# Attention scores as four 64x64 quarters without one block, and v's transfer issued first in its slot

## The chip, the cores and the metric

The kernel runs on one core of a Trainium2 chip. The metric is the device time of one execution in microseconds (us), taken as the median of several runs.

## The reference, cut to what matters

A linear attention with a decay per channel (4 batches, 8 heads, 768 steps, head size 48) feeds a soft mixture of experts (8 experts with 4 slots each, hidden size 1024). Everything is 32-bit floating point.

```python
for t in range(S):                                   # S = 768
    cur = einsum('bhd,bhe->bhde', u * kt, vt)
    y[:, :, t] = einsum('bhd,bhde->bhe', rt, state + cur)
    state = wt[..., None] * state + einsum('bhd,bhe->bhde', kt, vt)
x = y.transpose(0, 2, 1, 3).reshape(B * S, H * D)    # 3072 x 384
logits = x @ phi                                     # 3072 x 32
d = softmax(logits, axis=0); c = softmax(logits, axis=1)
h = relu((d.T @ x)[e] @ w1[e]); slot_out[e] = h @ w2[e]
out = c @ slot_out
```

Step t reads the state of the steps before it, and its own key and value with the factor u. In chunks of 128 steps, the part inside a chunk is a product of scores: a key takes part for a query only if it is earlier than the query. So a 128 x 128 block of scores (keys down, queries across) is used above the diagonal alone, and of its four 64 x 64 quarters the one of late keys and early queries is not used at all.

## The kernel before

The work goes through 16 slots, n = 0 to 15, and a last one that only finishes (n = 16). A slot is one pair of heads of one batch: batch b = n // 4, pair j = n % 4. On the partitions, the two heads of a pair lie at rows 0 to 47 and 64 to 111. The kernel's order on each engine is the order in which the program writes it; no scheduler moves anything.

For each slot TensorE does, in this order: transposes of k (`b_kn`, L558); the output of the slot before, from the states (`c_inter`, L625) and from the scores and v (`c_av`, L634); the bonus with u (`b_bonus`, L583, not in slots with j = 3); the sums of k and v per chunk (`b_u`, L591, which reads the slot's v); and the scores in two halves of three chunks (`b_scores`, L569). Between the halves stand pieces of the experts' routing (L73, L77, L109 to L120). In slot 0 the first half of the scores stands ahead of the transposes, and where j is 2 the sums stand behind the first half.

A half of the scores is six matmuls: for each of three chunks and each of two heads, 48 rows, 128 keys as weights and 128 queries as moving columns. The heads use different row halves of the array and different banks of `ap`. The trace records each 32-bit matmul as two weight loads and two matmuls. Behind each half ScalarE copies `ap` (`b_at`, L574), GpSimd sets all but the part above the diagonal to zero (L576), and `c_av` of the next slot reads the result, in quarters of 64 weight columns.

VectorE makes the decayed keys and queries by scans (L526 to L544) for one unit of heads after another, ahead of their use. SyncE issues all DMAs, in program order; an issue that has to wait holds back those behind it. At a slot's head it issues, where the slot has them: the gather of the fourth pair's rows (`a_gather`, L511), which waits for VectorE; w of a later unit (`a_load_w`, L499), and its k and r (`a_load_kr`, L503); v of the next slot (`v_load`, L506), into one of three buffers; and pieces of the experts' weights (`weight_piece`, L670). At the kernel's start VectorE clears some tiles (L701 to L706) before its first scan.

After slot 16 come the last softmax, both expert layers and the mixing (L895 onward); a second program behind a test (`recompute`) is not entered.

Of the kernel before, what the change touches and what calls it, by code (L numbers as in the profile page):

```python
# [17 lines left out]
P = 128  # L18
# [3 lines left out]
B, H, S, D = 4, 8, 768, 48  # L22
# [3 lines left out]
NIT = B * NG  # L26
# [7 lines left out]
PIT = P + 1  # L34
# [15 lines left out]
def rwkv_soft_moe(ctx: ExitStack, tc: tile.TileContext, wc, krc, vc, cst, w1, w2, out):  # L50
    nc = tc.nc
# [397 lines left out]
    ap = [app[:, n] for n in range(2)]  # L449
# [38 lines left out]
    def Kt(n):  # L488
        b, g = divmod(n, NG)
        t = kr4[(NU * b + g) % 4] if g < NU else kr3  # L490
        return t[:, 0:RO]

    def Rt(n):
        b, g = divmod(n, NG)
        t = kr4[(NU * b + g) % 4] if g < NU else kr3
        return t[:, RO:KRW]

    def a_load_w(u):
        nc.sync.dma_start(out=ws[u % 2], in_=wc[u])  # L499

    def a_load_kr(u):
        for lo, hi in ((0, RO), (RO, KRW)):
            nc.sync.dma_start(out=kr4[u % 4][:, lo:hi], in_=krc[u][:, lo:hi])  # L503

    def v_load(n):
        nc.sync.dma_start(out=vts[n % 3].rearrange("p c h d -> p (c h d)"), in_=vc[n])  # L506

    def a_gather(u):
        s = u % NU
        for h in range(2):  # L510
            nc.sync.dma_start(out=kr3[64 * h + 16 * s:64 * h + 16 * s + 16, :],  # L511
                              in_=kr4[u % 4][64 * h + D:64 * h + 64, :])
# [10 lines left out]
    def a_back(u, lo=0, hi=ROW):  # L523
        w = ws[u % 2]
        n = (hi - lo) // PIT
        nc.vector.tensor_tensor_scan(out=G[:, lo:hi][:, ::-1], data0=w[:, lo:hi][:, ::-1],  # L526
                                     data1=g_one.broadcast_to([P, hi - lo]),
                                     initial=1.0, op0=ALU.mult, op1=ALU.min)
        nc.vector.reciprocal(out=holes(w, lo, n), in_=holes(Gp, lo + 1, n))
        if hi == ROW:  # L530
            later.append(lambda: nc.gpsimd.tensor_copy(out=chk[:, u, 0, :], in_=holes(w, 0)))
# [5 lines left out]
    def a_fwd(u, lo=0, hi=ROW):  # L537
        nc.vector.tensor_tensor_scan(out=G[:, lo:hi], data0=ws[u % 2][:, lo:hi],  # L538
                                     data1=g_zero.broadcast_to([P, hi - lo]),
                                     initial=1.0, op0=ALU.mult, op1=ALU.add)  # L540

    def a_r(u, lo=0, hi=ROW):
        r = kr4[u % 4][:, RO + lo:RO + hi]
        nc.vector.tensor_tensor(out=r, in0=r, in1=G[:, lo:hi], op=ALU.mult)  # L544
# [4 lines left out]
    def b_pat(n):  # L549
        src = holes(Kt(n), PIT, C - 1)  # L550
        nc.scalar.copy(out=pats[n % 2][:, :, 1:C],
                       in_=src.rearrange("p (o c) -> p o c", o=1).broadcast_to([P, D, C - 1]))
# [11 lines left out]
    def b_scores(n, hf):  # L564
        kt, rt = Kt(n), Rt(n)
        for cc in range(3):
            c = 3 * hf + cc
            for h in range(2):
                nc.tensor.matmul(  # L569
                    out=ap[h][:, cc * P:(cc + 1) * P], lhsT=kt[64 * h:64 * h + D, c * PIT + 1:c * PIT + PIT],  # L570
                    rhs=rt[64 * h:64 * h + D, c * PIT:c * PIT + P], start=True, stop=True)

    def b_at(n, hf):
        nc.scalar.copy(out=ats[n % 2][hf].rearrange("p h c t -> p h (c t)"), in_=app[:, :, 0:384])  # L574
# [20 lines left out]
    def b_a(n):  # L595
        if n % NG < NU:
            nc.scalar.copy(out=asb[n % 2], in_=aP)
# [76 lines left out]
    def weight_piece():  # L674
        for n, a in [next(pieces, (None, None))]:
            if n is None:
                return
            if n < E:
                in_halves(wa[n], w1[n], a * F, (a + 1) * F)
            else:  # L680
                in_halves(wa[n], w2[n - E], FT * COLS[a][0], FT * COLS[a][1])
# [22 lines left out]
    nc.vector.memset(g_zero, 0.0)  # L704
    nc.vector.memset(siT[:, 0:8], 0.0)
    nc.vector.memset(tp[0], 0.0)  # L706
    nc.gpsimd.memset(ones, 1.0)
    for n in range(2):
        nc.gpsimd.memset(pats[n], 0.0)
# [14 lines left out]
    for n in range(NIT + 1):  # L724
        b, j = divmod(n, NG)
        live = n < NIT
        m, l = n - 1, n - 2
        lb, lj = divmod(l, NG)
        sb_ = b - 1
        soft = live and 0 <= sb_ < B - 1  # L730

        u_next = NU * (b + 1) + j - 1
        if n == 0:
            a_load_w(2)
            a_load_kr(2)
        if j == 1 and live:
            a_gather(NU * b)
        if j in (1, 2) and live:
            a_gather(NU * b + j)
        if j >= 1 and u_next < B * NU and live:  # L740
            a_load_w(u_next)
            a_load_kr(u_next)
        if n + 1 < NIT:
            v_load(n + 1)
        if live:
            for _ in range(PIECES[n]):
                weight_piece()

        u0 = NU * b
        nxt = b + 1 < B  # L750
        if live:
            b_pat(n)
            if n == 0:
                a_back(1)
            elif j == 0:
                a_fwd(u0 + 1)
                a_r(u0 + 1)
                a_chk(u0 + 1)
            elif j == 1 and b:
                a_k(u0 + 2)  # L760
                a_fwd(u0 + 2)
            elif j == 2 and nxt:
                a_back(u0 + 3)
            elif j == 3 and nxt:
                a_r(u0 + 3)
                a_chk(u0 + 3)
        if n == NIT:
            q = qs[b - 2]
            sp0 = tp[0][0:TG, 0:DM]
            s_mm(xb[b % 2], q, sp0)  # L770
            l_turn(l, app)
            l_mm(0, xTs[0], lpv, True, False)
            s_acc(b - 2, q, sp0)
            s_sum(b - 2, q)
            s_rows_exp(q)
            s_norm(b - 2, q)

        if n == 0:
            b_scores(n, 0)
            b_at(n, 0)  # L780
        if live:
            b_kn(n)
        if m >= 0:
            c_inter(m)
            c_av(m)
            c_evac(m, n == NIT)
        if live:
            b_bonus(n)
        if n == 0:
            a_rk(1)  # L790
        elif live and j != 1 and (j == 0 or nxt):
            a_rk(u0 + (2 if j == 0 else j + 1))
        if live:
            if n == 1:
                keep_warm(2, tp[1])
            if j != 2:
                b_u(n)
            if n:
                b_scores(n, 0)
                b_at(n, 0)  # L800
            if j == 2:
                b_u(n)
            b_state(n)
            b_a(n)
        if j == 0 and b > 1 and live:
            q = qs[b - 2]
            s_mm(xb[b % 2], q, spv)
            s_acc(b - 2, q, spv)
            s_sum(b - 2, q)
        if soft and j == 1:  # L810
            l_mm(0, xTs[0], lpv, True, False)
            l_mm(1, xTs[1], lpv, False, True)
            nc.scalar.copy(out=lt_t, in_=lpv)
        if soft and j == 2:
            l_mm(2, xTs[0], lpv, True, True)
            nc.vector.tensor_tensor(out=lt_t, in0=lt_t, in1=lpv, op=ALU.add)
            qs[sb_] = q = s_max(sb_, lt_t)
        if soft and j == 3:
            s_turns(qs[sb_], dpv, lnv)

        if live:
            if n == 0:
                a_k(1)
                a_fwd(1)
                a_r(1)
                a_chk(1)
            if j == 0:
                a_back(u0 + 2)
            elif j == 1:
                if b == 0:  # L830
                    a_k(u0 + 2)
                    a_fwd(u0 + 2)
                a_r(u0 + 2)
                a_chk(u0 + 2)
            elif j == 2 and nxt:
                a_k(u0 + 3)
                a_fwd(u0 + 3)
            elif j == 3 and nxt:
                a_back(u0 + 4)
                a_k(u0 + 4)  # L840
        if live:
            b_tc(n)
        if l >= 0 and lj >= 1 and live:
            l_turn(l, ypp)
        if n == 1:
            keep_warm(4, tp[1])
        if live:
            b_scores(n, 1)
            if n == 1:
                keep_warm(2, tp[1])  # L850
            b_at(n, 1)
            b_av(n)
            while later:
                later.pop(0)()
            if n == 0:
                a_rk(2)
                keep_warm(9, yb[0])
        if soft and j == 2:
            s_exp(sb_, q)
        if j == 0 and 1 < b and live:  # L860
            s_rows_exp(qs[b - 2], nc.gpsimd)
        if j == 1 and 1 < b:
            ce = qs[b - 2]["ce"]
            nc.scalar.activation(out=ce, in_=ce, func=AF.Exp)
            s_norm(b - 2, qs[b - 2], nc.gpsimd)
# [205 lines left out]
```

## Time and profile before

| what | value |
|---|---|
| runs | 202.03 us median of 3 (192.95 to 204.23) |
| profiled execution | 194.6 us, its span 192.7 us |
| granted TensorE clock over the span | 0.955 |
| DMA | 52.12 MB, 270 GB/s over the span |
| slots 0 to 2 | to about 34 us |
| slots 3 to 15 | about 34 to 134 us |
| the last slot, experts and mixing | 134 to 192.7 us |

The profile is of one execution. Its span is from the first to the last instruction; the execution's time has 1.9 us more around it. PE is TensorE's matmuls and PEld its weight loads, which overlap them. In the chain of waits each row is a start, a length and what ended last there. "issue" is time in which an engine stood without waiting for anything that the profile shows. SPq is SyncE's queue of DMA issues. The queue q8 of the DMA table carries instructions, not data.

### The profile page before, as it was taken

The numbers are of one execution on the slowest core, as the hardware profiler recorded it, in microseconds if no ns is written. First come the engines' busy times: TensorE is split into PE (matmuls) and PEld (weight loads), VectorE is DVE, ScalarE is ACT, GpSimd is POOL, SyncE is SP. The second block draws the span as 40 slices with busy tenths as digits, with TensorE's granted clock in tenths as the row PEclk, the third lists the DMA queues.
The fourth block names the chain that finished last, engine by engine and source line by source line (L and its number), as shares of the span: only waits on it lengthen the run. The fifth ranks groups of instructions, "written<-read, shape, count | busy, mean of one in ns | idle before, by whom it ended". The sixth has DMA issues, their size and how long they took to land.

```text
span 192.7 us, 7876 instructions
## 1 busy us (share of the span) xinstructions
PE 169.2 (88%) x3393; PEld 126.5 (66%) x3397; DVE 110.1 (57%) x181; ACT 83.5 (43%) x187; POOL 87.5 (45%) x129
## 2 busy tenths in 40 slices
PE   6969999798899997999789999999979898998650
PEld 2464878787878984878679688896433225787450
DVE  4889497889564994947977691425431400124520
ACT  4233165375394672665546648674030201022420
POOL 5354667966639876539486576567000000000000
PEclk9975999999999999999999999999999999999955
DMA  5996748999999899999969998999995593008672
GB/s 135 340 323 177 200 154 221 379 385 376 246 373 310 305 316 376 255 383 275 340 197 336 354 266 228 315 379 377 363 360 173 209 264 121 0 3 359 260 284 99
DMA packets 23849, 52.12 MB, mean 270 GB/s; under 512 B 2944, under 2 KB 6784, under 8 KB 23808
## 3 DMA queue, kind: packets, MB, share of 16 engines
q1 hardware_dynamic: 23808, 51.55, 80.3%
q8 instruction: 28, 0.46, 1.1%
q14 instruction: 13, 0.11, 0.2%
HBM read 44.44 MB, written 4.72 MB: 255 GB/s over the span
## 4 chain that ended last, share of the span: by engine, by line
PE 74%; DMA 11%; DVE 4%; issue 3%; ACT 3%; POOL 0%; SPq 0%; DVEq 0%; ACTq 0%; POOLq 0%
PE ap L569 13%; PE y L634 10%; DMA v<-in_vc_dram 9%; PE G L197 6%; PE y L230 5%; PE y L625 5%; PE tp L591 5%; PE tp L558 4%; PE tp L583 4%; PE tp L77 3%; PE y L73 3%; PE ap L253 2%; PE tp L120 2%; DMA krb<-in_krc_dram 2%; PE y L687 2%
## 5 line engine op out<-in xcount | busy, mean ns | idle before, releaser
L576 POOL TENSOR_SCALAR_AFFINE_SELECT blkat<-blkat 128x768 f32<-128x768 f32 x32 | 27.7, 866 | 37.6 <-ACT blkat L574 28.4
L574 ACT COPY blkat<-ap 128x768 f32<-128x768 f32 x32 | 25.7, 802 | 29.0 <-PE ap L569 27.4
L634 PE MATMUL y<-v,blkat 128*64 128x48 f32 x768 | 26.1, 224 | 0.0
L569 PE MATMUL ap<-krb 48*128 48x128 f32 x288 | 23.7, 295 | 1.9 <-issue 1.4
L634 PEld LDWEIGHTS y<-v,blkat 128*64 128x64 f32 x768 | 23.8, 138 | 1.1
L569 PEld LDWEIGHTS ap<-krb 48*128 48x128 f32 x288 | 18.9, 192 | 5.9 <-ACT blkat L574 2.6
L526 DVE TENSOR_TENSOR_SCAN G<-blkw,G 128x774 f32<-128x774 f32 (+1 forms) x13 | 21.3, 1637 | 1.5 <-DMA blkw<-in_wc_dram 1.3
L538 DVE TENSOR_TENSOR_SCAN G<-blkw,G 128x774 f32<-128x774 f32 (+1 forms) x13 | 21.5, 1651 | 0.5
L519 POOL TENSOR_TENSOR blka<-krb 128x768 f32<-128x768 f32 x11 | 17.1, 1554 | 1.2 <-DMA krb<-in_krc_dram 1.2
L600 DVE TENSOR_TENSOR_SCAN Traw<-tp,blkm 112x288 f32<-112x288 f32 x16 | 12.1, 754 | 9.0 <-PE tp L591 9.0
L647 DVE TENSOR_TENSOR x<-y,av 128x288 f32<-128x288 f32 x17 | 7.6, 452 | 12.7 <-ACT x L644 11.5
L616 POOL TENSOR_TENSOR av<-v,asb 128x576 f32<-128x576 f32 x12 | 14.1, 1178 | 0.0
L591 PE MATMUL tp<-v,blkm 128*48 128x48 f32 x320 | 11.2, 215 | 3.1 <-DMA v<-in_vc_dram 2.4
L645 POOL TENSOR_TENSOR x<-x,av 128x288 f32<-128x288 f32 x15 | 12.0, 801 | 2.4 <-ACT x L644 1.9
L230 PE MATMUL y<-wa,x 128*32 128x160 f32 (+1 forms) x144 | 12.2, 274 | 0.4 <-issue 0.4
L197 PE MATMUL G<-wa,siT 128*32 128x512 f32 x96 | 11.3, 597 | 1.1 <-ACT x L204 0.8
L544 DVE TENSOR_TENSOR krb<-krb,G 128x774 f32<-128x774 f32 (+1 forms) x13 | 11.6, 894 | 1.1 <-POOL blka L519 0.8
L591 PEld LDWEIGHTS tp<-v,blkm 128*48 128x48 f32 x320 | 9.3, 129 | 4.5 <-DMA v<-in_vc_dram 1.5
L644 ACT COPY x<-y 128x288 f32<-128x288 f32 x15 | 6.0, 399 | 13.8 <-PE y L634 13.8
L535 DVE TENSOR_TENSOR krb<-krb,G 128x774 f32<-128x774 f32 (+1 forms) x13 | 11.6, 889 | 0.7 <-DMA krb<-in_krc_dram 0.4
L583 PE MATMUL tp<-cst,blka 128*64 128x4 f32 x288 | 10.3, 200 | 1.6 <-ACT blkm L562 1.6
L687 PEld LDWEIGHTS <-siT 128*128 128x128 bf16 x53 | 5.4, 114 | 9.3 <-issue 5.1
(160 smaller groups left out, 329.6 us busy)
## 6 DMA issues: line engine op xcount, KB each, us to landing
wa<-in_w_dram SPq DMA_DIRECT2D x50, 256.0 KB, 6.1
v<-in_vc_dram SPq DMA_DIRECT2D x16, 288.0 KB, 6.0
krb<-in_krc_dram SPq DMA_DIRECT2D x11, 387.5 KB, 5.5
blkw<-in_wc_dram SPq DMA_DIRECT2D x11, 387.0 KB, 5.2
krb<-in_krc_dram SPq DMA_DIRECT2D x11, 387.0 KB, 6.0
out_dram<-wa SPq DMA_DIRECT2D x4, 960.0 KB, 4.8
krb<-in_w_dram SPq DMA_DIRECT2D x8, 320.0 KB, 6.0
blka<-krb SPq DMA_DIRECT2D x24, 96.8 KB, 6.2
```

The costliest lines, as they stand in the source:

```text
L197: nc.tensor.matmul(out=hp[32 * g:32 * g + NS, :], lhsT=siT[:, e * KT + kt, :], rhs=wts[e][:, kt * F + hf * 512:kt * F + hf * 512 + 512], s ...
L230: nc.tensor.matmul(out=so[32 * g:32 * g + NS, :], lhsT=hT[ft // 2][:, ft % 2, e, :], rhs=w2_at(e, cg, ft), start=((st_, ft) == (0, 0)), st ...
L519: nc.gpsimd.tensor_tensor(out=rks[u % 2][:, c0:c0 + cn_], in0=k3, in1=r3, op=ALU.mult)
L526: nc.vector.tensor_tensor_scan(out=G[:, lo:hi][:, ::-1], data0=w[:, lo:hi][:, ::-1], data1=g_one.broadcast_to([P, hi - lo]), initial=1.0, ...
L538: nc.vector.tensor_tensor_scan(out=G[:, lo:hi], data0=ws[u % 2][:, lo:hi], data1=g_zero.broadcast_to([P, hi - lo]), initial=1.0, op0=ALU.m ...
L569: nc.tensor.matmul(out=ap[h][:, cc * P:(cc + 1) * P], lhsT=kt[64 * h:64 * h + D, c * PIT + 1:c * PIT + PIT], rhs=rt[64 * h:64 * h + D, c * ...
L574: nc.scalar.copy(out=ats[n % 2][hf].rearrange("p h c t -> p h (c t)"), in_=app[:, :, 0:384])
L576: nc.gpsimd.affine_select(out=at, in_=at, pattern=[[0, 6], [1, P]], compare_op=ALU.is_gt, fill=0.0, base=0, channel_multiplier=-1)
L583: nc.tensor.matmul(out=aP[p:p + 64, c, :], lhsT=rks[(NU * b + g) % 2][:, c, p:p + 64], rhs=ub[:, g, :], start=True, stop=True)
L591: nc.tensor.matmul(out=U[64 * h:64 * h + D, :, c + 1], lhsT=kn[:, h, c, :], rhs=vt[:, c, h, :], start=first[h], stop=(c == C - 2))
L616: nc.gpsimd.tensor_tensor(out=avs[n % 2], in0=vts[n % 3].rearrange("p c h d -> p h c d"), in1=a.rearrange("p c (h o) -> p h c o", o=1).bro ...
L634: nc.tensor.matmul(out=yb[h][p:p + 64, c * D:(c + 1) * D], lhsT=ats[n % 2][c // 3][:, h, c % 3, p:p + 64], rhs=vt[:, c, h, :], start=False ...
```

## The change

It has two parts. In `b_scores` each matmul of 128 keys becomes two of 64 keys: the early keys (`p` = 0) against all 128 queries, the late keys (`p` = 64) against the late 64 queries. With two heads, the quarters stand on four 64 x 64 parts of the array. The block of late keys and early queries is no longer written, so two memsets at the start give those rows of `ap` a defined value. And `v_load(n + 1)` moves from behind the slot's gather and its loads of w, k and r to the slot's head.

```diff
@@ b_scores
             for h in range(2):
-                nc.tensor.matmul(
-                    out=ap[h][:, cc * P:(cc + 1) * P], lhsT=kt[64 * h:64 * h + D, c * PIT + 1:c * PIT + PIT],
-                    rhs=rt[64 * h:64 * h + D, c * PIT:c * PIT + P], start=True, stop=True)
+                for p in range(0, P, 64):
+                    nc.tensor.matmul(
+                        out=ap[h][p:p + 64, cc * P + p:(cc + 1) * P],
+                        lhsT=kt[64 * h:64 * h + D, c * PIT + 1 + p:c * PIT + 65 + p],
+                        rhs=rt[64 * h:64 * h + D, c * PIT + p:c * PIT + P], start=True, stop=True)
@@ the start
     nc.vector.memset(tp[0], 0.0)
+    for n in range(2):
+        nc.vector.memset(ap[n][64:P], 0.0)
     nc.gpsimd.memset(ones, 1.0)
@@ the loop over slots
         u_next = NU * (b + 1) + j - 1
+        if n + 1 < NIT:
+            v_load(n + 1)
         if n == 0:
             a_load_w(2)
             a_load_kr(2)
...
             a_load_w(u_next)
             a_load_kr(u_next)
-        if n + 1 < NIT:
-            v_load(n + 1)
         if live:
```

On TensorE, slot 5 from the bonus to the next slot's transposes, before; a row is a line, an operation, what it writes and reads, the output's shape and how many (`tp` holds the sums and the transposes, `y` and `tp_80` the routing):

```order
L583 MATMUL tp_79<-cst,blka 64x4 x12
L591 MATMUL tp_79<-v_101,blkm 48x48 x10
L569 MATMUL ap<-krb_91 128x128 x6
L77 MATMUL tp_80<-blkm,cst 32x256 x6
L73 MATMUL y<-cst,x_97 128x128 x6
L569 MATMUL ap<-krb_91 128x128 x6
```

The same place with the change, where each left-out part goes on with pairs like the two rows ahead of it, six pairs a half:

```order
L585 MATMUL tp_79<-cst,blka 64x4 x12
L593 MATMUL tp_79<-v_101,blkm 48x48 x10
L570 MATMUL ap<-krb_91 64x128
L570 MATMUL ap<-krb_91 64x64
...
L77 MATMUL tp_80<-blkm,cst 32x256 x6
L73 MATMUL y<-cst,x_97 128x128 x6
L570 MATMUL ap<-krb_91 64x128
L570 MATMUL ap<-krb_91 64x64
...
```

A half has 12 matmuls in place of 6, an early quarter and a late one in turn; nothing else moved on TensorE.

On SyncE, the DMA issues of slots 1 and 2, before (`blkw` is w, `krb` k and r, `blka` the gathered rows, `v_99` to `v_101` v's three buffers, `wa` the experts' weights):

```order
L511 DMA blka<-krb_91 16x1549 x4
L499 DMA blkw<-in_wc_dram 128x774
L503 DMA krb_92<-in_krc_dram 128x775
L503 DMA krb_92<-in_krc_dram 128x774
L506 DMA v_101<-in_vc_dram 128x576
L511 DMA blka<-krb_92 16x1549 x2
L499 DMA blkw<-in_wc_dram 128x774
L503 DMA krb_91<-in_krc_dram 128x775
L503 DMA krb_91<-in_krc_dram 128x774
L506 DMA v_99<-in_vc_dram 128x576
L670 DMA wa_82<-in_w_dram 128x512 x4
```

And with the change:

```order
L506 DMA v_101<-in_vc_dram 128x576
L511 DMA blka<-krb_91 16x1549 x4
L499 DMA blkw<-in_wc_dram 128x774
L503 DMA krb_92<-in_krc_dram 128x775
L503 DMA krb_92<-in_krc_dram 128x774
L506 DMA v_99<-in_vc_dram 128x576
L511 DMA blka<-krb_92 16x1549 x2
L499 DMA blkw<-in_wc_dram 128x774
L503 DMA krb_91<-in_krc_dram 128x775
L503 DMA krb_91<-in_krc_dram 128x774
L672 DMA wa_82<-in_w_dram 128x512 x4
```

v of slots 2 and 3 now stands ahead of the gather and the three loads of its slot, directly behind what the slot before issued.

## The prediction, made before the change was timed

> **What bounds the kernel now.** I read the page first, then a table by stretches, then the chain of waits.
>
> ```profile
> span 192.7 us, 7876 instructions
> PE 169.2 (88%) x3393; PEld 126.5 (66%) x3397; DVE 110.1 (57%) x181; ACT 83.5 (43%) x187; POOL 87.5 (45%) x129
> PE 74%; DMA 11%; DVE 4%; issue 3%; ACT 3%; POOL 0%; SPq 0%; DVEq 0%; ACTq 0%; POOLq 0%
> ```
>
> TensorE (PE, with PEld for its weight loads) is busy 88% of the span and holds 74% of the chain that ended last; no other engine is over 57%. DMA has 11% of the chain, and 3% is "issue", time in which the engine waited for nothing that the profile shows. The slots from n = 3 to the end lie in this stretch:
>
> ```profile
> 34.00:134.00 100.00, 94.42 (x2184) 78.73 (x2184) 68.31 (x92) 59.33 (x131) 67.72 (x96) 1.00 0.98 322
> ```
>
> Its columns are the length, then busy time and count of PE, PEld, DVE, ACT and POOL, the granted clock, the DMA share and GB/s. PE is busy 94 of 100 us at full clock, and the DMA engines are busy 98% of the time. So the kernel goes at TensorE's pace, and what TensorE lacks is the time it does not compute. One part is waiting for v; the other shows in the chain around slot 10:
>
> ```profile
> 51.16 0.54 issue
> ...
> 91.67 0.42 PE ap L569 x4
> 92.10 1.39 issue
> 93.49 0.72 PE ap L569 x7
> 94.20 0.63 PE tp L558 x5
> 94.83 0.73 PE y L625 x40
> 95.56 1.54 PE y L634 x48
> 97.09 0.45 PE tp L591 x20
> 97.54 0.53 PE ap L569 x5
> 98.07 0.82 issue
> 98.89 0.27 PE ap L569
> ```
>
> All three stops fall in the middle of a run of equal matmuls, where nothing is awaited. Between the last two lie 7 + 5 + 40 + 48 + 20 + 5 = 125 matmuls in the chain's count, each with its weight load: about 250 instructions. The instruction queue's row for 33.9 to 133.5 us (packets, MB, share) gives the same unit:
>
> ```profile
> q8 instruction: 17, 0.28, 1.2%
> ```
>
> 2184 + 2184 instructions of TensorE over 17 packets are 257 a packet. I read the stops as TensorE at the end of one packet with the next not there yet. Together they are 0.54 + 1.39 + 0.82 = 2.75 us. From the end of the second to the end of the third, 93.49 to 98.89, are 5.40 us: that is what a packet takes when TensorE waits for it. Today a packet's instructions last 100 / 17 = 5.88 us on average, so most fetches are just covered.
>
> **The scores.** Before, a half (three chunks, two heads) is 6 matmuls, recorded as 12 in two passes, each with 128 weight columns against 128 moving columns; the two heads sit on different row halves of the array and run side by side, so a half is 6 steps. What sets a step is read by comparison with other shapes:
>
> ```profile
> 52.35 0.87 PE ap L569 x12
> 53.22 0.99 PE tp L77 x12
> 145.50 2.78 PE G L197 x24
> ```
>
> L77 runs 3 column strips side by side with 256 moving columns, so 4 steps of 0.248 us; L197 runs 4 strips with 512, so 6 steps of 0.463 us. The difference is 0.215 us for 256 columns: 0.84 ns a column. 128 columns are 0.107 us, six steps of them 0.65 us of the 0.87; the rest is the start and the end. The change keeps, for the early keys, all 128 queries as moving columns; only the late keys go down to 64. Early and late quarters use different column halves, and stand beside each other as four-quarter matmuls do in L625 (row below). So a half still streams 6 times 128 columns on its longest quarter: the skipped block is streaming time that was never on the longest one. What does shrink is the first weight load, 64 columns in place of 128:
>
> ```profile
> L569 PE MATMUL ap<-krb x2: 373/374/374, 52.3 to 52.3; 48*128 48x128 f32 x2
> L569 PE MATMUL ap<-krb x288: 266/272/579, 7.6 to 123.5; 48*128 48x128 f32 x144
> L634 PE MATMUL y<-v,blkat x768: 222/222/257, 19.7 to 134.9; 128*64 128x48 f32 x192
> L625 PE MATMUL y<-Tc,krb x480: 200/218/255, 19.0 to 125.0; 48*64 48x48 f32 x160
> ```
>
> The first matmuls of a half last 374 ns against a median of 272, 102 more; with 64 weight columns the first ones last 257 against 222, 35 more. That is 67 ns a half, and 32 halves are **-2.1 us**. The bounds: nothing, if the start is hidden, and 0.102 x 32 = -3.3 us, if it all goes.
>
> **More instructions.** The 192 score matmuls become 384. The trace holds 384 matmuls and 384 loads for 192 (288 + 96 of each), so 768 instructions are added. In the stretch 34 to 134 us lie 13 slots, 26 halves of 24 more: 624, or 2.4 packets on top of 17.
>
> Without the three stops (2.75), the wait for v (2.4, next part) and 26 starts (1.7), the stretch would need 100 - 2.75 - 2.4 - 1.7 = 93.1 us for 19.4 packets, 4.80 us each. That is under the 5.40 us which a packet takes when awaited. So TensorE would catch up with its instructions at most packets, and the stretch goes at 19.4 x 5.40 = 104.8 us: **+4.8 us**, in which the gains inside the stretch are already used up. Bounds of this term: all new packets hidden, 93.1 + 2.75 = 95.9, so -4.1; or each packet as slow as today's mean of 5.88, 114.1, so +14.1. I take 5.40 because it is the one interval in which TensorE did wait at both ends, and because the DMA share of 0.98 does not let me expect a shorter one.
>
> The Trainium skill, "Runtime: NRT & Kernel Launch", section "Instruction fetch mechanics", says that instructions come in blocks of 16 KiB, 256 of them, while the block before is executed, and that the cost of crossing is "mostly hidden". The trace agrees with the block (257 a packet) and not, at three crossings, with the hiding; the sum by the page's rule is the first rival's.
>
> **The transfer of v.** SyncE's issues of the three late ones (slots 3, 4 and 8) and of what stands ahead of them, the median from issue to landing, and the three waits:
>
> ```profile
> 21.91 0.43 SPq L506 DMA_DIRECT2D v<-in_vc_dram  x1
> 27.62 1.15 SPq L511 DMA_DIRECT2D blka<-krb  x2
> 28.87 0.53 SPq L499 DMA_DIRECT2D blkw<-in_wc_dram  x1
> 31.16 0.38 SPq L506 DMA_DIRECT2D v<-in_vc_dram  x1
> 31.60 2.23 SPq L670 DMA_DIRECT2D wa<-in_w_dram  x4
> 37.35 1.40 SPq L506 DMA_DIRECT2D v<-in_vc_dram  x1
> 59.53 2.56 SPq L670 DMA_DIRECT2D wa<-in_w_dram  x4
> 67.49 0.38 SPq L506 DMA_DIRECT2D v<-in_vc_dram  x1
> v<-in_vc_dram SPq DMA_DIRECT2D x16, 288.0 KB, 6.0
> 36.56 0.34 PE L591 MATMUL tp<-v,blkm 128*48 128x48 f32 x6 [1.06 <-DMA v<-in_vc_dram]
> 43.93 0.25 PE L591 MATMUL tp<-v,blkm 128*48 128x48 f32 x2 [0.39 <-DMA v<-in_vc_dram]
> 73.34 0.60 PE L591 MATMUL tp<-v,blkm 128*48 128x48 f32 x17 [0.96 <-DMA v<-in_vc_dram]
> PE tp L591 <- DMA v<-in_vc_dram: 2.4, 3, 1.1
> ```
>
> SyncE is free at 22.3 but stands until 27.62 at the gather, which waits for VectorE, and issues v of slot 3 only at 31.16. At the head of the slot it goes out near 22.4, with its buffer last read by slot 0's matmuls, done by then; 6 us later it is there, at 28.5 for a use at 35.5. The other two can go when the weights ahead of them are issued, at 33.8 in place of 37.35 and at 62.1 in place of 67.49, which is 3.5 and 5.4 us earlier against waits of 0.39 and 0.96. So **-2.4 us**; bounds 0 and -2.4, as these waits are all there are. Behind v on SyncE the gather and the loads of w, k and r are issued 0.4 us later; they wait for VectorE there anyway, and in this trace TensorE waits for none of them in the loop. In slots with no such cover the 0.4 us would come off their lead.
>
> **The two memsets** on VectorE at the start take at most twice this one's time, in this gap:
>
> ```profile
> 1.64 0.48 DVE L706 MEMSET tp<- 128x512 f32 x1
> 3.43 0.97 DVE L526 TENSOR_TENSOR_SCAN G<-blkw,G 128x387 f32<-128x387 f32 x1 [1.30 <-DMA blkw<-in_wc_dram]
> ```
>
> 0.97 us in an idle 1.30: nothing. Without the gap they would cost 1 us.
>
> **Sum.** Stretch +4.8; six halves outside of it, 6 x 0.067 = -0.4; the span goes from 192.7 to 197.1. The profiled execution took 194.6 us in all, 1.9 more than its span, so **199.0 us**. The runs shown have a median of 202.03 (192.95 to 204.23): the profiled one is near their lower end, and the same 4.4 us on the median would give 206.4.
>
> **Rivals.**
> First, the instructions stay hidden: faster. The packets come early enough, as 14 of 17 do now, and only the gains count: -2.4 - 2.1 = -4.5, **190.1 us**. For it: three stops in 17 packets. Against it: the stops stand in the densest slots, and every slot gets denser by 48 instructions. It decides as soon as an awaited packet takes under 4.8 us.
> Second, the two draw level: at 5.16 us a packet 19.4 packets take 100 us and the time stays at **194.6**, within 2%.
> Third, the quarters do not run side by side, since they differ in moving columns. Then the late quarters' 64 columns (half of 0.65 us) are added to each half: 32 x 0.32 = +10.3, less 2.4 for v: **202.5 us** before any fetch is counted. Against it: L625's 40 matmuls take 0.73 us, 18 ns each with 48 moving columns, which only four at a time can do.
>
> **Chances.** Forecast 0.50 (0.33 slower by over 2%, and 0.17 within, where the packet takes 5.2 to 5.37 us); first rival 0.30 (0.23 faster, 0.07 within, where some of the gain is lost); second 0.14; third 0.06, slower. Together faster 0.23, within 2% 0.38, slower 0.39; 2%, some 4 us, is about what a measurement of this kernel can tell. The range reaches from the first rival, 190, to a stretch at 5.88 us a packet, 194.6 + 14.1 - 0.4 = 208, which also takes in the forecast on top of the runs' median. The likeliest case alone has 196 to 203.
>
> **What would show it.** Right: some 20 packets in the same stretch; "issue" stops of 0.5 us and more at five or more places, about 128 matmuls apart; no wait for v; score halves of 0.80 us where no stop falls in. Wrong: as few stops as now (first rival); halves of 1.1 us or more without a stop (third); a wait for w, k or r in place of v, which I hold to be absent.

## The result, and the profile after the change

| | before | after |
|---|---|---|
| median of 5 runs | 193.67 us (192.49 to 204.23) | 200.78 us (199.68 to 206.13) |
| ratio, with its 95% interval | | 1.0385 [1.0323, 1.0447] |
| profiled execution, its span | 194.6 us, 192.7 us | 201.52 us, 199.5 us |

The change makes the kernel 3.9% **slower**, about 7 us. The comparison leaves disturbed executions out, and since the changed kernel's first profile fell in one, its lines below are from a second profile. The page, in the three rows that answer to those of before:

```profile
span 199.5 us, 8634 instructions
PE 169.3 (85%) x3777; PEld 123.2 (62%) x3781; DVE 111.9 (56%) x183; ACT 83.6 (42%) x187; POOL 87.3 (44%) x129
PE 81%; issue 8%; DVE 4%; ACT 3%; ACTq 0%; DVEq 0%
```

TensorE has 768 more instructions and the same busy time. DMA, with 11% of the chain before, has left it, and "issue" has gone from 3% to 8%: from 6.7 to 16 us of the span. The stretch that the prediction read, and the instruction queue's packets from 31.4 to 140.8 us, in which the same slots now lie:

```profile
34.00:134.00 100.00, 88.41 (x2296) 72.27 (x2296) 64.17 (x85) 54.08 (x119) 61.99 (x87) 0.97 0.91 299
```
```profile
q8 instruction: 20, 0.33, 1.2%
```

PE is busy 88 of 100 us instead of 94. There are 20 packets, as forecast. The stops of TensorE in the chain of waits, early slots:

```profile
28.18 0.65 issue
...
33.43 0.68 issue
...
39.26 1.05 issue
...
45.27 0.68 issue
...
50.09 0.41 issue
```

Five stops in a row end at 28.83, 34.11, 40.30, 45.95 and 50.50: 5.28, 6.19, 5.65 and 4.55 us apart, 5.42 on average. That is TensorE getting one packet of 256 instructions at a time and using it up before the next is there. The counts behind PE and PEld say so, for the first three intervals:

```profile
28.83:34.11 5.28, 4.43 (x128) 3.71 (x127) 4.65 (x5) 2.77 (x7) 3.64 (x7) 1.00 0.90 301
34.11:40.30 6.19, 4.97 (x128) 4.01 (x128) 5.69 (x7) 3.71 (x7) 4.96 (x6) 1.00 1.04 394
40.30:45.95 5.65, 4.78 (x128) 4.08 (x128) 4.50 (x6) 2.45 (x5) 3.44 (x5) 1.00 1.05 386
```

Each holds 128 matmuls and, to within one, 128 weight loads. In the trace's order of TensorE's instructions all 13 stops of the loop stand at one place modulo 256, to within one, and each ends 1.2 to 1.7 us after one of the queue's packets of 16,384 bytes has come. Later in the loop the same chain, around its second half:

```profile
80.09 1.54 PE y L636 x48
81.63 0.66 PE tp L585 x24
82.29 0.21 PE tp L593 x6
82.50 1.54 issue
84.05 0.56 PE tp L593 x14
84.61 0.81 PE ap L570 x17
85.42 1.46 PE tp L77 x12
86.87 1.47 PE y L73 x6
88.35 1.25 PE ap L570 x18
89.59 0.63 PE tp L558 x5
```

The stop splits a group of 20 equal matmuls in 6 and 14. L77 behind it takes 1.46 us where it took 0.99 before, and the score half at 88.35 takes 1.25 where the one at 84.61 takes 0.81. The table by stretches says why; its last columns are clock, DMA share and GB/s:

```profile
82.40:85.81 3.41, 1.87 (x50) 1.35 (x48) 1.54 (x4) 0.27 (x1) 0.92 (x2) 1.00 1.04 388
85.81:89.22 3.41, 3.41 (x37) 2.27 (x33) 0.44 (x1) 2.27 (x5) 0.86 (x1) 0.50 0.68 139
```

The granted clock goes in pieces of 3.41 us. The piece with the stop had PE busy for 1.87 us; the next one has half the clock. I call that a cut piece; where TensorE sets the pace it costs half its length, 1.7 us. What TensorE waits for, by line:

```profile
PE ap L570 <- issue: 5.7, 5, 2.2
PE tp L593 <- issue: 4.9, 6, 1.5
...
PE y L636 <- issue: 1.9, 2, 1.0
```

The wait for v, 2.4 us before, has no row any more, and none for w, k or r has come.

### The profile page after: what moved, and what is told of

It reads as the page before. It is cut to its first block, busy times and chain, and to the rows that moved or that the text cites. A ratio compares the mean times of both kernels' runs of the same rounds, so it can differ in the third digit from the quotient of the medians.

```text
span 204.3 us, 8634 instructions
## 1 busy us (share of the span) xinstructions
PE 177.7 (87%) x3777; PEld 130.5 (64%) x3781; DVE 111.5 (55%) x183; ACT 83.9 (41%) x187; POOL 87.4 (43%) x129
## 4 chain that ended last, share of the span: by engine, by line
PE 80%; issue 6%; DVE 4%; ACT 3%; DMA 2%; POOL 0%; SPq 0%; ACTq 0%; DVEq 0%; POOLq 0%
PE ap L570 14%; PE y L636 14%; PE y L627 6%; PE G L197 5%; PE y L230 5%; PE tp L593 5%; PE tp L558 5%; PE tp L585 4%; PE tp L77 4%; PE y L73 4%; PE tp L120 2%; DMA krb<-in_krc_dram 2%; PE ap L253 2%; ACT blkat L576 2%; PE y L689 1%
## 5 line engine op out<-in xcount | busy, mean ns | idle before, releaser
L636 PE MATMUL y<-v,blkat 128*64 128x48 f32 x768 | 29.8, 240 | 0.0
L570 PE MATMUL ap<-krb 48*64 48x128 f32 (+1 forms) x576 | 24.0, 269 | 5.1 <-issue 4.5
L636 PEld LDWEIGHTS y<-v,blkat 128*64 128x64 f32 x768 | 27.4, 154 | 1.3
L570 PEld LDWEIGHTS ap<-krb 48*64 48x64 f32 x576 | 17.2, 141 | 9.6 <-issue 6.2
L593 PE MATMUL tp<-v,blkm 128*48 128x48 f32 x320 | 12.4, 224 | 4.1 <-issue 4.0
L593 PEld LDWEIGHTS tp<-v,blkm 128*48 128x48 f32 x320 | 10.3, 138 | 5.7 <-issue 5.1
L646 ACT COPY x<-y 128x288 f32<-128x288 f32 x15 | 6.0, 399 | 18.4 <-PE y L636 18.4
L544 DVE TENSOR_TENSOR krb<-krb,G 128x774 f32<-128x774 f32 (+1 forms) x13 | 11.6, 893 | 1.3 <-POOL blka L519 0.9
L585 PE MATMUL tp<-cst,blka 128*64 128x4 f32 x288 | 10.8, 202 | 1.6 <-ACT blkm L562 1.6
L535 DVE TENSOR_TENSOR krb<-krb,G 128x774 f32<-128x774 f32 (+1 forms) x13 | 11.6, 889 | 0.7 <-POOL blka L519 0.6
```

Of the source, the lines that this page charges most:

```text
L570: nc.tensor.matmul(out=ap[h][p:p + 64, cc * P + p:(cc + 1) * P], lhsT=kt[64 * h:64 * h + D, c * PIT + 1 + p:c * PIT + 65 + p], rhs=rt[64 * ...
L585: nc.tensor.matmul(out=aP[p:p + 64, c, :], lhsT=rks[(NU * b + g) % 2][:, c, p:p + 64], rhs=ub[:, g, :], start=True, stop=True)
L593: nc.tensor.matmul(out=U[64 * h:64 * h + D, :, c + 1], lhsT=kn[:, h, c, :], rhs=vt[:, c, h, :], start=first[h], stop=(c == C - 2))
L636: nc.tensor.matmul(out=yb[h][p:p + 64, c * D:(c + 1) * D], lhsT=ats[n % 2][c // 3][:, h, c % 3, p:p + 64], rhs=vt[:, c, h, :], start=False ...
```

## The experiments

**Theory 1**: each packet of TensorE's instructions costs about 5.4 us when awaited, because the experts' weights keep the DMA busy beside it, and the change needs more packets. **Theory 2**: the quarters cost by themselves, as matmuls. **Theory 3**: v's earlier transfer pushes other loads back. Times are medians; the runs of the kernel before that were taken on the same chip stand beside them. In the first group of four, all seven of these had a granted clock of 0.865 to 0.904 and a median of 203.24 us (201.19 to 210.84), so there the level of before is another one; the sixth experiment looks for the reason.

### 1. v at the head of the slot alone

```
         u_next = NU * (b + 1) + j - 1
+        if n + 1 < NIT:
+            v_load(n + 1)
...
-        if n + 1 < NIT:
-            v_load(n + 1)
```

> The kernel before with v's transfer issued at the head of the slot and nothing else. Theory 1 (what costs is the fetch of TensorE's instructions; v's earlier transfer is a gain): the three waits for v, 2.4 us, go, and since the instructions are as many as before some of that comes back at the stops for them: 0.985 to 0.998 of the time before, 191 to 193.3 us. Theory 3 (v's earlier transfer pushes other loads back and that is what costs): 1.01 or more, with a new wait for w, k, r or the gather in the waits.

Measured: 196.44 us (195.43 to 201.31), ratio 0.966 [0.958, 0.975]. No wait for v is left, nor a new one for a load. Theory 3 falls. The gain is larger than the 2.4 us forecast, because of the level of before in this group.

### 2. The quarter scores alone

```
-                nc.tensor.matmul(
-                    out=ap[h][:, cc * P:(cc + 1) * P], ...
+                for p in range(0, P, 64):
+                    nc.tensor.matmul(
+                        out=ap[h][p:p + 64, cc * P + p:(cc + 1) * P], ...
```

> The kernel before with the quarter scores alone; v is issued where it was. 768 instructions more on TensorE. Theory 1 (instruction fetch): slower by as much as both edits together or more, 1.035 to 1.05 of the time before, with issue stops of 0.4 to 2 us in the middle of runs of equal matmuls, one at nearly each 256 instructions, and the score halves themselves no longer than 0.87 us. Theory 2 (the quarters themselves are slower steps): the halves last over 1 us where no stop falls in. Theory 3 (v's transfer costs): within 1% of the time before.

Measured: 203.37 us (202.95 to 207.73), ratio 1.002 [0.995, 1.008]: by the ratio a miss for theory 1, against a kernel before at its upper level. Against v alone, in the same group, it is 6.9 us slower, but that pair differs in both edits. The pair that differs in the quarters alone is v alone and the changed kernel (the fourth experiment), and there the quarters cost 5.5 us. What TensorE waits for in this run:

```profile
PE tp L593 <- issue: 6.2, 4, 2.4
PE ap L570 <- issue: 3.2, 3, 2.4
PE tp L593 <- DMA v<-in_vc_dram: 2.1, 1, 2.1
```

The stops of the change are there without its other edit, 9.4 us of them in two rows.

### 3. Empty instructions in place of quarters

```
                     rhs=rt[64 * h:64 * h + D, c * PIT:c * PIT + P], start=True, stop=True)
+                for _ in range(4):
+                    nc.tensor.nop(hint="pad", nofuse=True)
```

> The kernel before with its whole 128x128 scores and v where it was, and 24 empty instructions for TensorE in each half of the scores, four behind each matmul: 768 in all, as many as the quarters add, and nothing more to compute. Theory 1 (the number of instructions is what costs): as slow as the quarters alone, 1.035 to 1.05, with stops 256 instructions apart, plus what an empty instruction takes in the queue, which shows as score halves longer than 0.87 us and is to be taken off. Theory 2 (the quarters as matmuls cost, by their shape or by the clock gate's reaction to them): within 1% of the time before, apart from what the longer halves show.

Measured: 226.95 us (226.06 to 227.57), ratio 1.118 [1.111, 1.125]. Three score halves of its chain, all at full clock:

```profile
88.55 1.43 PE ap L569 x11
...
92.20 0.87 PE ap L569 x12
...
108.47 1.35 PE ap L569 x12
```

The empty instructions are not free: most halves are 0.4 us and more above 0.87. The loop then lasts so long that most packets come in time, and TensorE's stops are 6 us in all. The run does not tell theories 1 and 2 apart; a load of empty instructions is no neutral stand-in here.

### 4. The changed kernel again

> The changed kernel once more, beside the others on one chip, for a second profile of it. All theories: 1.03 to 1.045 of the time before. Theory 1: five or more issue stops at steps of 256 instructions, and behind the longer stops TensorE's granted clock falls to half for some microseconds, as in the first profile. If the halved clock belongs to that one execution alone, this profile has the stops with a clock of 1.0 between 34 and 134 us.

Measured: 201.96 us (201.52 to 204.63), ratio 0.995 [0.988, 1.001] against the 203.24 of this group. This is the profile shown above: 13 stops, 12.5 us together, and two cut pieces from 34 to 134 us (clock 0.97). So the changed kernel is where it was, 200 to 202 us; the kernel before had moved.

### 5. Fewer columns, the same instructions; and all columns

The first of the two (diag) streams 64 columns in each quarter, so it leaves out the block of early keys and late queries, which is set to zero at the start; the second (full) streams 128:

```
-                        out=ap[h][p:p + 64, cc * P + p:(cc + 1) * P],
+                        out=ap[h][p:p + 64, cc * P + p:cc * P + p + 64],
...
-                        rhs=rt[64 * h:64 * h + D, c * PIT + p:c * PIT + P], ...
+                        rhs=rt[64 * h:64 * h + D, c * PIT + p:c * PIT + p + 64], ...
```
```
-                        out=ap[h][p:p + 64, cc * P + p:(cc + 1) * P],
+                        out=ap[h][p:p + 64, cc * P:(cc + 1) * P],
...
-                        rhs=rt[64 * h:64 * h + D, c * PIT + p:c * PIT + P], ...
+                        rhs=rt[64 * h:64 * h + D, c * PIT:c * PIT + P], ...
```

> The changed kernel with the early keys against the early queries alone too, so that all four quarters stream 64 columns; the block of early keys and late queries is left out of the computation (zero). As many instructions as the change. Theory 2 (what the scores stream sets the time): 32 halves less 0.33 us each, 10 us under the changed kernel, about 190 us. Theory 1 (the fetch sets the time): score halves of 0.5 us, but the stops grow by nearly as much, and the time stays within 3 us of the changed kernel's 200 to 202 us.

> The changed kernel with the late keys against all queries, so that no block is skipped and all four quarters stream 128 columns; as many instructions as the change, and the reference's result. Prediction's reading (a half streams as long as its longest quarter, so the skipped block saves nothing): score halves of 0.80 us as in the changed kernel and its time within 1%. If the skipped block does save: halves of over 0.9 us and 3 to 10 us more than the changed kernel.

Measured: diag 201.62 us (198.05 to 202.46), full 204.84 us (201.48 to 207.77); no interval for either. A score half at full clock, of diag and then of full:

```profile
61.17 0.51 PE ap L570 x24
```
```profile
60.43 0.82 PE ap L570 x24
```

diag computes 0.30 us less in each of 32 halves, 9.6 us, and is no faster than the change: 198.05 at its best, 201.62 in the median. Its stops:

```profile
PE ap L570 <- issue: 6.9, 5, 2.6
PE tp L593 <- issue: 6.5, 5, 2.1
```

With a third row (0.8) they are 14.2 us, only 1.7 more than the change's 12.5. More of the 9.6 us went into cut pieces: six in the loop from 29 to 121 us in place of the change's two, which by half their length are 6.8 us more. So the median alone doesn't show that the saved time was waited out at the packets. A narrower comparison does speak for theory 1: four times both traces go at full clock from one stop to the next, one packet on, at the same place of the program. The change takes 5.65, 4.55, 4.37 and 5.30 us there, diag 5.64, 6.20, 5.20 and 5.04. Shorter matmuls don't make these stretches shorter. In full the half takes 0.82 against the change's 0.81 us, so the skipped block saves next to nothing, as the prediction read it.

### 6. The kernel before again

> The kernel before, for a second profile of it, since its runs stand at 193 us with a granted clock of 0.955 or at 203 us with 0.90. Theory 1 with the clock: TensorE's clock is set for pieces of 3.41 us by how busy TensorE was in the piece before; at 203 us the same stops for instructions and for v stand in the trace as at 193, and five to seven pieces of the loop behind them have half the clock. Against it: the clock is low in pieces with no stop ahead of them, which would make it a matter of the chip and not of the kernel.

Measured: 203.94 us (192.63 to 206.12): on one chip the same kernel took 192.63 with a clock of 0.961 and 203.55 in the profile, with 0.899. Its wait for v from 28 to 40 us, and two stretches of its table:

```profile
PE tp L591 <- DMA v<-in_vc_dram: 2.7, 2, 2.2
```
```profile
31.24:34.65 3.41, 1.89 (x64) 1.66 (x56) 2.63 (x3) 1.43 (x5) 3.20 (x6) 1.00 0.96 310
34.65:65.37 30.72, 30.07 (x388) 25.69 (x390) 16.05 (x17) 10.87 (x22) 11.84 (x16) 0.50 0.81 267
```

One wait for v of 2.2 us left PE 1.89 us of work in its piece, and nine cut pieces follow, though PE is busy through them. So the cut lies behind a wait of the kernel here, and its length, nine pieces against single ones in the changed kernel's profile above, is what moves this execution from 193 to 203 us. That the other executions at 203 us have the same cause is argued from this one trace and their clocks.

### 7. The weights out of the loop

```
-PIECES = (0, 0, 2, 2) + (2,) * 10 + (2, 1)
+PIECES = (0,) * 15 + (27,)
```

> The kernel before with all 27 pieces of the experts' weights issued in slot 15 in place of two a slot, so that the loop has only the loads of w, k, r and v beside it; the same result. Its end is later by the weights that are then awaited (14 MB, some 37 us at 380 GB/s), and only the loop is compared: from the first to the last eviction of scores it took 120.4 us in the kernel before. Theory 1 (a packet of instructions waits behind the loads): no issue stop over 0.3 us in the loop, no wait for v, and 120.4 - 2.75 - 2.4 = 115 us. Against it: the stops are still there, so they are not owed to the loads.

> The changed kernel with all 27 pieces of the experts' weights in slot 15, as in the run beside it. Theory 1: no stops in this loop either, though it has 768 instructions more, and the loop 1 to 3 us shorter than that of the kernel before with late weights (the shorter first weight loads, 2 us). Theory 2 (quarters or their number of instructions cost by themselves): a loop longer by 5 us or more, as it is with the weights beside it.

Measured, one execution each, the evictions of the scores (count, durations, first and last start) and the loop by stretches, first of before with late weights and then of the change with late weights:

```profile
L574 ACT COPY blkat<-ap x32: 796/800/862, 9.3 to 125.5; 128x768 f32<-128x768 f32 x32
```
```profile
34.00:119.00 85.00, 82.73 (x1949) 69.67 (x1946) 64.40 (x85) 51.67 (x115) 60.79 (x87) 1.00 0.62 183
```
```profile
L576 ACT COPY blkat<-ap x32: 799/800/842, 9.6 to 125.8; 128x768 f32<-128x768 f32 x32
```
```profile
34.00:119.00 85.00, 83.27 (x2295) 68.65 (x2296) 62.81 (x84) 53.61 (x119) 61.00 (x86) 1.00 0.64 193
```
What TensorE waited for in these two loops, from 20 to 125 us:

```profile
PE tp L591 <- DMA v<-in_vc_dram: 1.9, 3, 1.2
```
```profile
PE tp L593 <- issue: 3.7, 3, 2.2
PE ap L570 <- issue: 0.8, 1, 0.8
PE y L636 <- issue: 0.5, 1, 0.5
```

With the weights in the loop the evictions span 120.7 us before (9.7 to 130.4) and 127.8 after (9.8 to 137.6): 7.1 more. Without them both span 116.2, and the two kernels are level. That the two numbers are equal is partly luck: before has two cut pieces at the start (11.4 to 18.2) which the change has not, and the change loses as much at the end, where the weights begin. From the third eviction to the second of slot 14, where neither falls, they take 95.2 and 95.1 us; with the weights in the loop the same stretch took 99.8 and 108.6, the latter with two cut pieces in it. The loop of before has no stop of TensorE left. It still waits for v, 1.9 us, so the expectation that the weights alone delay v missed. The change keeps 5.0 us of stops in place of 12.5, the largest (2.2, at 119 us) where the 27 pieces have begun to move (the first is issued at 109.2), so that no stop at all was a miss too, and so was a loop shorter by 1 to 3 us. The weights' traffic, then, is the larger part of what the stops cost: at a DMA share of 0.62 to 0.64 in place of 0.91 to 0.98 the change's loss is gone. Even there it needs its packets a little faster than they come in the early slots: 2.8 us of stops lie between 28 and 60 us.

### 8. v alone again, and with weights moved

```
-PIECES = (0, 0, 2, 2) + (2,) * 10 + (2, 1)
+PIECES = (0, 0, 2, 2, 2, 2, 2, 2, 1, 1, 1, 2, 2, 2, 2, 4)
```

> The kernel before with v at the head of the slot, once more. In its first profile three pieces of 3.41 us at half clock in the loop cost 5 us, so its gain did not show against the faster executions of the kernel before. Theory 1: where no piece of the loop is at half clock it takes 190 to 192 us, 2 to 3 us less than the 192 to 194 of the kernel before in such executions; and fewer of its runs than of the kernel before stand above 200 us, since the longest waits are gone.

> The kernel before with v at the head of the slot, and three of the 27 weight pieces moved from slots 8 to 10 to slot 15: the stops at 92 and 98 us stand in those slots. Theory 1: fewer and shorter stops between 70 and 100 us, 1 to 2 us gained on v at the head of the slot alone, unless the end now waits for weights: three pieces are 1.5 MB, 4 us of the loads, for which the DMA has about half of 134 to 144 us free. Against it: the stops stay, and the end is later by up to 4 us.

Measured beside 12 runs of before with a median of 197.31 us (192.18 to 205.97): v alone 193.23 us over 10 runs (190.01 to 199.88), ratio 0.991 [0.980, 1.002]; with the weights moved 192.5 us over 4 runs (190.05 to 194.4), ratio 0.989 [0.964, 1.015]. One of the 10 runs of v alone had a granted clock under 0.91, four of the 12 of before did. v alone is the best version found, and the plain ratio leaves open whether it wins anything where no cut is set off; that three pieces elsewhere add to it is not shown.

### 9. Half the instructions, and fewer with dearer matmuls

```
-                for p in range(0, P, 64):
+                w = 64 if hf == 1 else P
+                for p in range(0, P, w):
```

(for half0, `hf == 0`); and, in the joined form:

```
-            for p in range(0, P, 64):
-                nc.tensor.matmul(out=aP[p:p + 64, c, :], lhsT=rks[(NU * b + g) % 2][:, c, p:p + 64],
-                                 rhs=ub[:, g, :], start=True, stop=True)
+            nc.tensor.matmul(out=aP[:, c, :], lhsT=rks[(NU * b + g) % 2][:, c, :],
+                             rhs=ub[:, g, :], start=True, stop=True)
```

> The changed kernel with quarters in the second half of the scores alone; the first half is whole, 128 by 128. 384 instructions more than before instead of 768, v at the head of the slot. Theory 1 (each packet more costs, about 5 us in the loop that the weights run beside): halfway between v at the head alone (190 to 193 us where the clock is not cut in the loop) and the changed kernel (199.7 to 201.5): 194 to 197 us. If the cost came from the first few instructions over some limit, all of it would stand here already: 199 us or more.

> As the run beside it, with the quarters in the first half of the scores alone: the same number of instructions at another place of the slot. Theory 1: 194 to 197 us, as beside. If the place decides (how dense the instructions of one packet stand), the two differ by more than 2 us.

> The changed kernel with the bonus matmuls of 64 weight columns, two for each chunk, joined to one of 128 columns: 288 instructions fewer on TensorE, 1.1 packets of 256, the same result. Joined, six steps a slot load 128 columns in place of 64, by the score's columns some 0.05 us more each, 0.3 us in each of 12 slots, 4 us in all. Theory 1 (the loop goes at the pace of the packets): 1.1 packets of 5.4 us fewer, 3 to 6 us under the changed kernel's 200 to 202 us. Theory 2 (matmul time sets it): 3 to 4 us over it.

> The changed kernel with the joined bonus matmuls, once more: its first profile had an eleven-piece stretch at half clock, which hides what the stops cost. 288 instructions fewer than the change, 4 us more matmul time by estimate. Theory 1: the sum of the stops in the loop falls from the changed kernel's 10 to 12 us to 6 to 8 us, and about the same comes on in matmul time, so 199 to 202 us where the loop is not at half clock. If fewer instructions bring nothing: 203 us or more with stops of 10 us.

> The changed kernel, as what the three beside it are compared with on one chip. All theories: 199.5 to 202 us where the loop is not at half clock for more than two or three pieces, 9 to 12 us of stops.

Measured, the last group of four beside before at 199.84 us (192.96 to 209.11): half1 202.23 (195.45 to 205.34), half0 203.68 (197.35 to 208.61), the changed kernel 201.28 (198.39 to 208.11), ratio 1.033 [1.009, 1.056]. The lowest runs of the halves lie between those of v alone and of the change, as theory 1 has it, but it is one run each with no interval; the medians hang on cut pieces, five of them behind one stop in half1:

```profile
41.03 2.39 issue
```
```profile
40.24:43.66 3.42, 1.03 (x38) 0.94 (x35) 1.36 (x2) 0.40 (x1) 1.50 (x4) 1.00 1.05 393
43.66:60.72 17.06, 17.06 (x234) 14.11 (x232) 9.27 (x10) 6.09 (x13) 6.48 (x9) 0.50 0.91 273
```

So the dose is not settled in size. The joined form took 211.5 us (201.55 to 217.25) and 208.78 us (206.44 to 213.94, ratio 1.081 [1.055, 1.107]), a miss for the forecast of 199 to 202. Its stops, and its bonus group at full clock:

```profile
PE ap L570 <- issue: 4.8, 3, 2.1
```
```profile
57.70 1.43 PE tp L584 x12
```

The stops did shrink, from 12.5 us to 5.5 with the other row (0.7), but the bonus takes 1.43 us a slot where it took 0.66: some 9 us in 12 slots, not the estimated 4. Fewer instructions were bought too dear.

## Why the prediction was wrong

**The step that failed first is the last one of the sum**, where 194.6 + 4.4 became 199.0 and the runs' median of 202.03 was set aside with "the profiled one is near their lower end". Against the time shown of before, 199.0 reads as 1.5% faster, while the text argues for slower. Of the three runs shown, two lay at the upper level, at which later runs of before had a granted clock of about 0.90, and the profiled execution lay at the lower, with 0.955. The comparison settles before at 193.67, next to the profile, so the base was the right one; what failed is that a gap of 9 us between runs was left unexplained, and the number and the chances hung on it. A forecast needs to say which level of before it is against.

**The size**: +4.4 us forecast, +6.8 between the two profiled spans, +7.1 between the medians. The term that was mis-sized is the stretch of 104.8 us: the same slots took 109.4 (31.4 to 140.8 us; in the kernel before 99.6, from 33.9 to 133.5). The sum let all its packets go at 5.40 us. For 14 of the 19 from the first stop to the last this was right: they took 75.5 us, 5.39 each. The other five, from 84.05 to 113.81 us, took 29.8 us, 5.95 each, and there lie the two cut pieces, of which the sum had not thought. Most of the rest of the 4.6 us lies behind the last stop, from 134.05 us on, where TensorE is busy throughout and its matmuls, not the packets, set the pace. Luck made part of the miss good: the change enters the stretch 2.5 us earlier (31.4 against 33.9), because the kernel before has two cut pieces ahead of it (11.6 to 18.4) and the change none.

The same +7.1 counted by what TensorE did, from the first to the last eviction of scores, where the whole of it lies:

| term | forecast | measured |
|---|---|---|
| stops for packets | 104.8 - 93.1 = 11.7 in the stretch, 2.75 before | 12.5 from 28 to 134 us, 3.1 before with one of 0.34 in slot 0: +9.4 |
| wait for v | -2.4 | no row left: -2.4 |
| starts of score halves | -0.067 each, -2.1 in all | 0.87 to 0.81 us: -0.06 each, -1.9 in all |
| cut pieces | not thought of | two before, two after: about 0 over the whole |
| groups of matmuls that a stop breaks up | not thought of | 3.0 us more of TensorE's time, 0.9 before: +2.1 |

The sum of the right column is +7.2. So the mechanism was **right**, and so was the price of an awaited packet: 5.40 forecast, 5.42 measured over the four intervals above and 5.36 over all seven places where two stops stand one packet apart (4.37 to 6.19).

The last row needs a word. Twelve of the 13 stops fall inside a group of equal matmuls, and a group in two pieces keeps TensorE busy for longer than a whole one. An interval from stop to stop holds this time already; the forecast's matmul time of 93.1 us did not. The sums of k and v, broken up and whole:

```profile
33.09 0.34 PE L593 MATMUL tp<-v,blkm 128*48 128x48 f32 x7
34.11 0.51 PE L593 MATMUL tp<-v,blkm 128*48 128x48 f32 x13 [0.68 <-issue]
...
41.96 0.63 PE L593 MATMUL tp<-v,blkm 128*48 128x48 f32 x20
```

That is 0.85 us of busy time for the same 20 matmuls that take 0.63 otherwise; over the twelve it is 0.2 to 0.4 us each. It fits the count of the whole loop: TensorE's busy time from the first to the last eviction is 112.65 us before and 113.36 after (0.7 of the difference are transposes of slot 0 that fall inside only after), though the score halves are shorter. The ends of matmuls are modelled in the profile, so the size of this term is rough. The cut pieces cancel in this pair of traces alone; in the first profile of the change and in half1 they do not.

**The skipped block** saves nothing: right (full against the change, 0.82 and 0.81 us). **The memsets**: no wait for them shows; right. **The third rival**, quarters that do not run side by side, is out: the half is 0.81 us, not 1.1. **The first rival**, instructions that stay hidden, needs a packet under 4.8 us, and **the second**, a draw, one of 5.16; the four intervals average 5.42. The Trainium skill, "Runtime: NRT & Kernel Launch", section "Instruction fetch mechanics", has the crossing of a block as mostly hidden; the change's traces show 5.0 us of stops at a DMA share near 0.6 and 12.5 at 0.91, so it depends on what else the DMA moves.

## What to carry to other kernels

Count instructions as a load on the DMA: where TensorE lives on small matmuls and the DMA queues are full, a block of 256 instructions that is used up faster than it is fetched sets the pace, and matmul time saved there may win nothing: diag computes 9.6 us less and is no faster, with somewhat longer stops and more cut pieces behind them. Splitting a matmul pays only if its longest part gets shorter by more than the added instructions cost, so look at the interval between stops first. And when runs of a kernel lie at two levels, find out from the granted clock which waits make the upper one before a change is forecast against either.

## What the runs showed of the hardware that was not expected

- A stop much shorter than a clock piece mostly halves TensorE's clock. In the rows above, pieces of 3.41 us with PE busy for 1.87, 1.89 and 1.03 us are followed by half the clock; a piece with 2.02 us (90.10 to 93.51 in the kernel before) was not, nor one with 1.78 (82.33 to 85.74 in the second run of the joined form). The Trainium skill, "TensorE: Matmul & The Clock Gate", section "Why this matters for your kernels", warns of idle gaps over about 3 us; here stops of 1.5 to 2.4 us do it, so the measurement goes further than the page.
- A cut lasted one piece in one place and nine in another (30.72 us at 0.50), with PE busy for 30.07 of the 30.72. What ends it was not tried and stays open.
- Empty instructions on TensorE mostly cost time: score halves of 1.35 and 1.43 us in place of 0.87 with 24 of them between the matmuls, some 20 to 23 ns each there; the half at 92.20 took 0.87 with them.
- The transfer of a packet is the smaller part of its price. In the four intervals of 4.55 to 6.19 us it takes 1.0 to 1.2 us and begins 1.8 to 3.8 us after the stop before has ended; what fills the time ahead of it is not shown.
- Twelve records of joined bonus matmuls, 128 weight columns before 4 moving ones, take 1.43 us, 119 ns each, where 24 records of 64 columns took 0.66 us. Their weight loads are busy for 1.41 us of it, so I read the load as what sets the pace.
